# A gated mix of a state-space scan and an FFN on one core: the first x by DMA transposes, B's first slots loaded at once, and another order of the products

## The chip, the core and the metric

The kernel runs on one core of a Trainium2 chip. The time is the device time of one execution in microseconds (us). Before the change, three runs took 143.34, 143.43 and 144.09 us, a median of 143.43 us.

The engines are named as the profile names them: PE is TensorE's matmuls and PEld its weight loads, DVE is VectorE, ACT is ScalarE, POOL is GpSimd and SP is SyncE, which here only issues DMAs. All times in this document are in us unless ns is written.

## The reference

For 2048 tokens `x` of 448 values the kernel computes a gate, a diagonal complex recurrence (S5) over the tokens, an FFN with SiLU, and mixes the two:

```python
g = sigmoid((x * gate_w).sum(-1, keepdims=True))
# a: state-space part
Lam_bar = exp(dt * Lam)                       # 448 complex numbers, dt = exp(log_dt)
B_bar = ((Lam_bar - 1.0) / Lam)[:, None] * B  # 448 x 448 complex
Bu = x @ B_bar.T
h[t] = Lam_bar * h[t - 1] + Bu[t]             # over the 2048 tokens
a = 2.0 * (h @ C.T).real + x * Dskip
# b: FFN, 448 -> 1792 -> 448
b = silu(x @ w1) @ w2
out = g * a + (1 - g) * b                     # bfloat16
```

## The kernel before

**Tiling.** The tokens are cut into four chunks of 512 (`CH`), each of four blocks of 128. The 448 complex states are laid out as seven slots of 128 rows: slots 0 to 2 and half of slot 3 hold the real parts, the other half of slot 3 and slots 4 to 6 the imaginary parts. An eighth slot of `U` and of `Gb` is slot 3 with its halves swapped.

**Per chunk.** Every chunk goes through these stages:

- *Products with 64 rows.* `bu(tc, s)` makes slot s of B times x, `f1(tc, fb)` makes one of 14 blocks of 128 FFN units. Both contract over 448 = 7 x 64 rows, so `step(ta, tb)` runs two of them as a pair, one in each half of PE's rows: eight matmuls of 64 rows and 512 columns that open the pair (`begin`), and six that close it (`end`, issued by `close()` when the next step has begun, or by a call of its own). There are 42 steps. What closes a pair adds the evictions: `U` by ACT or DVE (L631, L633), the FFN's SiLU by ACT into `aT` (L692).
- *Lanes* (`lanes(tc)`, all DVE but for the copies): `U` is turned by the tables `COS` and `SIN` (L652), seven real scans of 512 run over the tokens (L665), their results are copied to `Gb` by ACT (L671) or POOL (L669, the slots in `GP`), and turned back into `H` (L652). The state passed to the next chunk is `gin`, from small POOL and DVE operations.
- *FFN outputs.* `ffn2(tb)` makes one block of 128 tokens from 14 matmuls (L703), and ACT scales it by 1-g into `Tb` (L707).
- *Readouts.* `readout(tb)` multiplies `H` by the converted C, `CP`, with seven matmuls (L731), and DVE adds `tf`, which is x*D*g plus `Tb`, and stores it (L721, L735).
- `gates(tc)` makes g with PE (L774), ACT (L779) and POOL (L780, L781); `skip(tc)` multiplies x by D (L713).

**Before the first product.** x of chunk 0 is loaded as it lies (`xnat`, L356, first on SP), transposed by PE in four groups of four (`x_transposes`, L441) and copied to `xT` by DVE (L447) and ACT (L449). x of the later chunks comes by DMA transposes (`load_xt`, L370), two for a load: columns 0 to 383, and 320 to 447. B is loaded in four pieces into `Bnat` (in `Tb`'s place), transposed by PE (`b_transposes`, L468) and copied to `BT` by DVE (L477) and ACT (L475), for slots 0 and 1, then 4 to 6, then 2 and 3. Four rows of parameters (`prm`, loaded on ACT's queue) are transposed by PE (L487, L489) into `pc`; from it come the phases `ph`, the tables `SIN` and `COS` (DVE, POOL and ACT, L523 to L548), and the small factors: the turn by 512 tokens (`s8`, `c8`, `CC`, `SS`, `SX`) and the factors of C (`sc1`, `sc2`), made by a row of tiny POOL operations (L562 to L589). `idle(n)` runs matmuls on zeros (L425).

**C.** Two DMA transposes bring C into `CT` (L389, also in `Tb`'s place), and `readout_weights(k)` converts it with the small factors: two ACT operations (L757, L759) and two DVE operations (L761, L764) for each of k = 0 to 2, and eight PE transposes, one ACT and one DVE operation for k = 3.

**The order.** The program isn't run in the order of its lines. `Plan` collects every operation with its reads and writes, a cost in us and a priority. `Plan.order()` then places them in time by those costs: each engine takes the operation that can start first, and of equal ones that with the lowest priority number. Only PE keeps the order in which its operations were added; that order is written out by hand at the end of the function (L800 to L868). PSUM's eight banks are given out by the same planner. `Waits` then turns the result into one list for each engine with semaphore waits, and each engine runs its own list strictly in order. A wrong cost therefore changes nothing but the order; an operation placed too early blocks what stands behind it on its engine.

The hand-written order before begins so:

```python
BU(0, (0, 1))
b_transposes(B456, ["Bn3"], 0, False)
b_transposes(B456, ["Bn3"], 1, True)
b_transposes(B23, ["Bn0", "Bn1", "Bn2"], 0, False)
b_transposes(B23, ["Bn0", "Bn1", "Bn2"], 1, True)
gates(0)
BU(0, (4, 5), (6, 2))
step(bu(0, 3), f1(0, 7))
F1(0, (0, 8), (1, 9), (2, 10), (3, 11), (4, 12), (5, 13))
```

After chunk 0 it alternates: the steps of a chunk, its four FFN outputs, with the readouts of the chunk before in between.

Of the kernel before, what the change touches and what calls it, by code (L numbers as in the profile page):

```python
# [17 lines left out]
CH = 512  # L18
# [28 lines left out]
class Plan:  # L47
# [6 lines left out]
    SWITCH = 0.10  # L54

# [46 lines left out]
    def order(self):  # L102
# [28 lines left out]
        while len(done) < len(ops):  # L131
# [20 lines left out]
            if o.sem is not None:  # L152
                free[o.eng] = t + o.cost
                if o.bytes > 4096:
                    pipe = max(pipe, t + 1.5) + o.bytes / 260e3
                    o.end = pipe + 0.4
                else:
                    o.end = t + 3.4
            else:
                extra = 0.0  # L160
                if o.eng == "pe":
                    extra = self.SWITCH if o.rows != rows else 0.0
                    rows = o.rows
                free[o.eng] = o.end = t + o.cost + extra
# [97 lines left out]
def bass_gated_mix__ssm_conv_s5__dense_activation_silu__prompt_kernel(nc, A_x, A_Lambda_re, A_Lambda_im, A_B_re, A_B_im, A_C_re, A_C_im,  # L262
               A_log_dt, A_Dskip, B_x, B_w1, B_w2, gate_w, out):
    with ExitStack() as ctx:
# [90 lines left out]
        def load(q, dst, src, name, nbytes, prio, reads=()):  # L355
            P.add(q, lambda e: e.dma_start(dst, src), list(reads), [name], 0.55 if q == "sp" else 0.3, prio, sem(), nbytes)  # L356
# [9 lines left out]
        def load_xt(tc, n, prio, cost, reads=()):  # L366

            rows = slice(tc * CH, (tc + n) * CH)
            for k, (o, c) in enumerate(((slice(0, 3), slice(0, 384)), (slice(3, 4), slice(320, 448)))):
                P.add("sp", lambda e, o=o, c=c: e.dma_start_transpose(xT[:, o, rows], x2[rows, c]), list(reads),  # L370
                      [f"xT{t}{k}" for t in range(tc, tc + n)], cost[k], prio + k, sem(), n * CH * (1100, 500)[k])

        load_x(0, 0)
        load("sp", Bnat[:, 0:3, :], A_B_re[0:384, :].rearrange("(s p) d -> p s d", p=128), "Bn0", 384 * 896, 1)
        load("sp", Bnat[:, 4:7, :], A_B_im[0:384, :].rearrange("(s p) d -> p s d", p=128), "Bn3", 384 * 896, 2)
        load("sp", Bnat[0:64, 3, :], A_B_re[384:448, :], "Bn1", 64 * 896, 3)
        load("sp", Bnat[64:128, 3, :], A_B_im[384:448, :], "Bn2", 64 * 896, 4)
        for h, (c0, c1) in enumerate(((0, 384), (384, 896))):
            w = w1s[:, :, :].rearrange("p b (q f) -> p b q f", q=2)
            for b in range(3):  # L380
                load("sp", w[:, b, :, c0:c1], B_w1[128 * b:128 * b + 128, :].rearrange("p (q f) -> p q f", q=2)[:, :, c0:c1],
                     f"w1{h}{b}", 128 * 4 * (c1 - c0), 5 + h)
            load("sp", w[64:128, 3, :, c0:c1], B_w1[384:448, :].rearrange("p (q f) -> p q f", q=2)[:, :, c0:c1],
                 f"w1{h}3", 64 * 4 * (c1 - c0), 5 + h)
            load("sp", w1s[0:64, 3, c0:c1], B_w1[320:384, c0:c1], f"w1{h}4", 64 * 2 * (c1 - c0), 5 + h)
        load("sp", w2s[:, :, :], B_w2.rearrange("(fb p) d -> p fb d", p=128), "w2", F_FF * 896, 8)
        load_xt(1, 1, 9, (3.0, 5.0))
        def load_ct(k, dst, src, cost, prio):
            P.add("sp", lambda e: e.dma_start_transpose(dst, src), [], [f"Cn{k}"], cost, prio, sem(), 448 * 800)  # L389


        load_ct(0, CT[:, 0:3, :], A_C_re[:, 0:384], 2.0, 11)
        load_ct(1, CT[:, 3:6, :], A_C_im[:, 0:384], 2.0, 12)
# [3 lines left out]
        def late_loads():  # L397
            load_xt(2, 2, 16, (6.0, 1.4), ["Gb7a", "Gb7b"])
# [3 lines left out]
            for tc in range(1, NCH):  # L402
                load_x(tc, 18 + tc, ["Gb7b"])
# [11 lines left out]
        ACT(lambda e: e.preload_act_table(AF.Exp), [], ["tbl"], 1.3, 4)  # L415


        DVE(lambda e: e.memset(PB[:, 0, :], 0.0), [], ["PB0"], 0.2, 0)  # L418

        def idle(n):  # L420
# [6 lines left out]
            P.add("pe", mm, ["PB0"], [tk], 0.107 * n)  # L427

        idle(15)


        def x_transposes(h, n):

            tk = Ps()

            def mm(pe):
                for q in range(2):
                    for b in range(2):
                        o = (q * 2 + b) * 128
                        c = XCOL[2 * n + q]  # L440
                        r = pe.transpose(bk16(tk)[:, o:o + 128], xnat[:, 2 * h + b, c:c + 128], ident[:, :])  # L441
                return r
            P.add("pe", mm, ["xn0", "ident"], [tk], 0.24)
            dst = xT[:, 2 * n:2 * n + 2, 256 * h:256 * h + 256]
            src = lambda: bk16(tk)[:, 0:512].rearrange("p (q n) -> p q n", q=2)
            if n == 0:
                DVE(lambda e: e.tensor_copy(dst, src()), [tk], [f"xT00{h}"], 0.42, 0)  # L447
            else:
                ACT(lambda e: e.activation(dst, src(), AF.Copy), [tk], [f"xT01{h}"], act_cost(512), 0)  # L449

        for h in range(2):
            for n in range(2):
                x_transposes(h, n)

        def xr(tc):
            return [f"xT{tc}{k}" for k in (range(2) if tc else ("00", "01", "10", "11"))]

        def b_transposes(slots, reads, h, to_act):
# [11 lines left out]
            P.add("pe", mm, reads + ["ident"], [tk], 0.06 * 2 * n)  # L470
# [10 lines left out]

        prmn = [f"prm{k}" for k in range(4)]
# [9 lines left out]
        b_transposes(B01, ["Bn0"], 0, False)  # L492
        b_transposes(B01, ["Bn0"], 1, True)
        idle(2)
# [59 lines left out]
        DVE(lambda e: e.tensor_single_scalar(ph[:, 4:8], ph[:, 0:4], 512.0, ALU.mult), ["ph"], ["ph5"], 0.2, 12)  # L554
        DVE(nearest(phk[:, 4:8], ph[:, 4:8]), ["ph5"], ["phk5"], 0.2, 12)
        DVE(minus(ph[:, 4:8], ph[:, 4:8], phk[:, 4:8]), ["ph5", "phk5"], ["ph5"], 0.2, 12)
        ACT(lambda e: e.activation(s8[:, :], ph[:, :], AF.Sin, scale=TURN), ["ph", "ph5", "tbl"], ["s8"], 0.25, 12)
        ACT(lambda e: e.activation(pha[:, :], ph[:, :], AF.Abs), ["ph", "ph5", "tbl"], ["pha"], 0.25, 12)
        ACT(lambda e: e.activation(c8[:, :], pha[:, :], AF.Sin, bias=hpi[:, :], scale=-TURN), ["pha", "hpi", "tbl"], ["c8"], 0.3, 12)

        def pt(o, a, b, op, r, w):
            POOL(lambda e: e.tensor_tensor(o, a, b, op), r, w, 0.15, 20)  # L562
        nr, ni, m1, m2, inv, a1, a2, a3 = (c[:, :] for c in cw)
        pt(nr, rc[:, :], c8[:, 0:4], ALU.mult, ["rc", "c8"], ["nr"])
        POOL(lambda e: e.tensor_single_scalar(nr, nr, -1.0, ALU.add), ["nr"], ["nr"], 0.15, 20)
# [5 lines left out]
        POOL(lambda e: e.tensor_single_scalar(inv, inv, 2.0, ALU.mult), ["inv"], ["inv"], 0.15, 20)  # L571
# [8 lines left out]
        POOL(lambda e: e.tensor_copy(sc1[:, 0:3], a1[:, 0:3]), ["a1"], ["sc1"], 0.1, 20)  # L580
        pt(sc1[:, 3:4], a1[:, 3:4], sgn[:, :], ALU.mult, ["a1", "sgn", "sc1"], ["sc1"])
        POOL(lambda e: e.tensor_single_scalar(sc1[:, 4:7], a1[:, 0:3], -1.0, ALU.mult), ["a1", "sc1"], ["sc1"], 0.1, 20)
        POOL(lambda e: e.tensor_single_scalar(sc2[:, :], a3, -1.0, ALU.mult), ["a3"], ["sc2"], 0.1, 20)
        POOL(lambda e: e.tensor_copy(CC[:, 0:4], c8[:, 4:8]), ["c8"], ["CC"], 0.1, 14)
        POOL(lambda e: e.tensor_copy(CC[:, 4:7], c8[:, 4:7]), ["c8", "CC"], ["CC"], 0.1, 14)
        POOL(lambda e: e.tensor_copy(SS[:, 0:3], s8[:, 4:7]), ["s8"], ["SS"], 0.1, 14)
        POOL(lambda e: e.tensor_single_scalar(SS[:, 4:7], s8[:, 4:7], -1.0, ALU.mult), ["s8", "SS"], ["SS"], 0.1, 14)
        pt(SS[:, 3:4], s8[:, 7:8], sgn[:, :], ALU.mult, ["s8", "sgn", "SS"], ["SS"])
        POOL(lambda e: e.tensor_single_scalar(SX[:, :], SS[:, 3:4], -1.0, ALU.mult), ["SS"], ["SX"], 0.1, 14)  # L589

        def half_steps(pe, a, b, lo, hi, start):
            for i in range(len(lo)):
                for p0, (w, xc, tk, c0), k in ((0, a, lo[i]), (64, b, hi[i])):
                    r = pe.matmul(bk(tk), w[p0:p0 + 64, k, c0:c0 + 128], xT[p0:p0 + 64, k, xc:xc + CH],  # L599
                                  start=(start and i == 0), stop=(not start and i == 2))  # L600
            return r

        open_pair = []

        def step(ta, tb):

            (wa, xa, ca, ra, ea), (wb, xb, cb, rb, eb) = ta, tb
            a, b = Ps("pair"), Ps("pair")
            begin = lambda pe: half_steps(pe, (wa, xa, a, ca), (wb, xb, b, cb), (0, 1, 2, 3), (0, 1, 2, 3), True)
            end = lambda pe: half_steps(pe, (wb, xb, b, cb), (wa, xa, a, ca), (0, 1, 2), (0, 1, 3), False)  # L610
            reads = ra + rb

            def evict(a, b):
                ea(a)
                eb(b)
            P.add("pe", begin, reads, [a, b], 0.866, rows=64)
            if open_pair:
                close()
            open_pair.append((end, reads, a, b, evict))

        def close():
            end0, reads0, a0, b0, evict0 = open_pair.pop()
            P.add("pe", end0, reads0, [], 0.65, acc=[a0, b0], rows=64)
            evict0(a0, b0)

        GP = ((), (0, 1), (0, 1), ())


        def u_out(s, tk, on_dve=False):
            if on_dve:  # L630
                DVE(lambda e: e.tensor_copy(U[:, s, :], bk(tk)), [tk], [f"U{s}"], dve_cost(512), 2)  # L631
            else:
                ACT(lambda e: e.activation(U[:, s, :], bk(tk), AF.Copy), [tk], [f"U{s}"], act_cost(512), 4)  # L633

        def bu(tc, s):
            def evict(tk):
# [267 lines left out]
```

## Time and profile before

| | |
|---|---|
| median of three runs | 143.43 us (143.34 to 144.09) |
| the profiled execution | 143.92 us |
| its span, from the first instruction to the last | 142.0 us |
| PE busy, share of the span | 97% |
| DVE busy | 89% |
| ACT busy | 56% |
| POOL busy | 24% |
| first product starts | 7.88 us |
| HBM read, written | 6.25 MB, 1.84 MB |

The profile counts time from the first instruction. Its page gives busy times and the costliest groups of instructions; the chain of waits goes back from the last instruction to what released each; a timeline lists instructions of one engine by start and duration, merged where neighbours are alike, with the idle time before them in brackets. Matmuls are pipelined, so their durations overlap: the time that one costs in a row of many is the distance from start to start. For DMAs the profile tells when an engine issued one, how long the issue took and when it landed.

### The profile page before, as it was taken

Reading aid. Unit: us, or ns where it says so; the run is one execution under the profiler, and the core shown is the slowest. Engines: PE = TensorE matmul, PEld = TensorE weight load, DVE = VectorE, ACT = ScalarE, POOL = GpSimd, SP = SyncE. Lnnn points to the kernel's source line nnn. Section 1 sums busy time; section 2 is a strip of 40 time slices with the busy share of each in tenths; the row PEclk is TensorE's granted clock in tenths of the full one; section 3 lists DMA queues with packets and bytes.
Section 4 is the critical chain, followed back from the end, with each engine's and each line's share of the span. In section 5 each row is a group of like instructions: output and inputs, shape, how many; then the busy total and the mean of one; then the engine's idle time right before and its main releaser. Section 6 shows DMA issues by size and latency. Waiting matters only on the chain.

```text
span 142.0 us, 2706 instructions
## 1 busy us (share of the span) xinstructions
PE 137.6 (97%) x1069; PEld 70.6 (50%) x1069; DVE 126.1 (89%) x145; ACT 79.1 (56%) x148; POOL 34.2 (24%) x66
## 2 busy tenths in 40 slices
PE   6989999999999999999999999999999999999993
PEld 4855555544444544444555554444455555555552
DVE  0399999998899299999999999999999999899393
ACT  3386698798965494889811014898721355411100
POOL 7184000089009520443450002542000000000000
PEclk9999999999999999999999999999999999999999
DMA  4989969201947600101000102000001021000113
GB/s 133 331 258 290 314 133 201 33 0 39 239 103 188 229 5 0 37 0 42 2 31 1 41 29 69 18 18 5 0 30 34 0 69 37 31 1 32 32 65 99
DMA packets 21108, 11.44 MB, mean 81 GB/s; under 512 B 11492, under 2 KB 21096, under 8 KB 21096
## 3 DMA queue, kind: packets, MB, share of 16 engines
q1 hardware_dynamic: 21088, 11.27, 30.5%
q8 instruction: 8, 0.13, 0.4%
q14 instruction: 4, 0.03, 0.1%
q10 hardware_dynamic: 8, 0.00, 0.0%
HBM read 6.25 MB, written 1.84 MB: 57 GB/s over the span
## 4 chain that ended last, share of the span: by engine, by line
PE 96%; DVE 1%; ACT 1%; POOL 1%; issue 0%
PE ps L599 45%; PE ps L703 30%; PE ps L731 15%; PE ps L425 2%; PE ps L441 1%; PE ps L774 1%; ACT BT L475 1%; PE ps L468 1%; POOL cw L562 0%; DVE ot L735 0%; PE ps L751 0%; DVE PB L418 0%; POOL gwc L497 0%; DVE pc L495 0%; DVE cw L570 0%
## 5 line engine op out<-in xcount | busy, mean ns | idle before, releaser
L599 PE MATMUL ps<-xT,w1s 64*128 64x512 bf16 x392 | 47.4, 376 | 0.0
L703 PE MATMUL ps<-w2s,aT 128*128 128x448 bf16 x224 | 44.7, 352 | 0.0
L692 ACT ACTIVATE aT<-ps 128x512 bf16<-128x512 f32 x56 | 30.0, 601 | 5.3 <-PE ps L599 5.2
L599 PEld LDWEIGHTS ps<-xT,w1s 64*128 64x128 bf16 x392 | 21.0, 94 | 22.7 <-issue 0.7
L703 PEld LDWEIGHTS ps<-w2s,aT 128*128 128x128 bf16 x224 | 21.7, 98 | 20.3 <-issue 0.4
L665 DVE TENSOR_TENSOR_SCAN Gf<-rc,gin,PA 128x512 f32<-128x512 f32 x21 | 26.8, 1322 | 0.0
L599 PE MATMUL ps<-xT,BT 64*128 64x512 bf16 x196 | 25.9, 376 | 0.7 <-DVE ph L511 0.6
L707 ACT ACTIVATE Tb<-ps,g 128x448 bf16<-128x448 f32 x16 | 10.1, 633 | 28.0 <-PE ps L703 21.4
L731 PE MATMUL ps<-CP,H 128*128 128x448 bf16 (+1 forms) x119 | 23.2, 341 | 0.0
L671 ACT ACTIVATE Gb<-Gf 128x512 bf16<-128x512 f32 x24 | 14.7, 630 | 8.4 <-DVE Gf L665 8.3
L599 PEld LDWEIGHTS ps<-xT,BT 64*128 64x128 bf16 x196 | 10.7, 94 | 12.1 <-DVE phk L508 0.8
L731 PEld LDWEIGHTS ps<-CP,H 128*128 128x128 bf16 x119 | 11.5, 98 | 9.8 <-issue 0.4
L633 ACT ACTIVATE U<-ps 128x512 bf16<-128x512 f32 x24 | 13.3, 592 | 2.2 <-PE ps L599 2.2
L735 DVE SCALAR_TENSOR_TENSOR ot<-ps,g,tf 128x448 bf16<-128x448 f32 (+1 forms) x17 | 11.1, 650 | 3.2 <-issue 2.2
L669 POOL CAST Gb<-Gf 128x512 bf16<-128x512 f32 x4 | 6.1, 1518 | 23.0 <-DVE Gf L665 23.0
L721 DVE SCALAR_TENSOR_TENSOR tf<-xnat,g,Tb 128x448 f32<-128x448 bf16 x16 | 10.6, 674 | 0.1
L652 DVE TENSOR_TENSOR PB<-Gb,SIN 128x1536 bf16<-128x1536 bf16 (+1 forms) x8 | 8.6, 1087 | 1.2 <-ACT Gb L671 1.1
L652 DVE TENSOR_TENSOR PB<-U,SIN 128x2048 bf16<-128x2048 bf16 (+1 forms) x8 | 8.6, 1080 | 0.0
L652 DVE TENSOR_TENSOR PA<-U,COS 128x3584 bf16<-128x3584 bf16 x4 | 8.1, 2020 | 0.2
L652 DVE TENSOR_TENSOR PA<-PA,PB 128x3584 bf16<-128x3584 bf16 x4 | 8.1, 2018 | 0.0
L652 DVE TENSOR_TENSOR H<-PA,PB 128x3584 bf16<-128x3584 bf16 x4 | 8.1, 2014 | 0.0
L652 DVE TENSOR_TENSOR PA<-Gb,COS 128x3584 bf16<-128x3584 bf16 x4 | 8.1, 2014 | 0.0
(97 smaller groups left out, 100.5 us busy)
## 6 DMA issues: line engine op xcount, KB each, us to landing
xnat<-in_A_x_dram SPq DMA_DIRECT2D x4, 448.0 KB, 6.1
out_dram<-ot SPq DMA_DIRECT2D x15, 112.0 KB, 1.7
w2s<-in_B_w_dram SPq DMA_DIRECT2D x1, 1568.0 KB, 9.3
w1s<-in_B_w_dram SPq DMA_DIRECT2D x3, 256.0 KB, 4.6
w1s<-in_B_w_dram SPq DMA_DIRECT2D x3, 192.0 KB, 4.3
Gb<-Gb SPq DMA_DIRECT2D x8, 64.0 KB, 1.9
U<-U SPq DMA_DIRECT2D x6, 64.0 KB, 2.0
Tb<-in_A_B_re_dram SPq DMA_DIRECT2D x1, 336.0 KB, 3.7
```

Of the source, the lines that this page charges most:

```text
L599: r = pe.matmul(bk(tk), w[p0:p0 + 64, k, c0:c0 + 128], xT[p0:p0 + 64, k, xc:xc + CH], start=(start and i == 0), stop=(not start and i == 2))
L633: ACT(lambda e: e.activation(U[:, s, :], bk(tk), AF.Copy), [tk], [f"U{s}"], act_cost(512), 4)
L652: return DVE(lambda e: e.tensor_tensor(o, a, b, op), r, w, dve_cost(n, 2), prio)
L665: DVE(lambda e, s=s, b=b, init=init: e.tensor_tensor_scan(Gf[:, s, :], rc[:, b:b + 1].to_broadcast([128, CH]), PA[:, s, :], init, ALU.mult ...
L669: POOL(lambda e, s=s: e.tensor_copy(Gb[:, s, :], Gf[:, s, :]), [f"Gf{s}"], [f"Gb{s}"], 0.75, 8)
L671: ACT(lambda e, s=s: e.activation(Gb[:, s, :], Gf[:, s, :], AF.Copy), [f"Gf{s}"], [f"Gb{s}"], act_cost(512), 4)
L692: ACT(lambda e: e.activation(aT[tc % 2][:, fb, :], bk(tk), AF.Silu), [tk, "tbl"], [f"aT{tc % 2}_{fb}"], act_cost(512), 3)
L703: r = pe.matmul(bk(tk)[:, 0:D_MOD], aT[tc % 2][:, fb, o:o + 128], w2s[:, fb, :], start=(fb == 0), stop=(fb == NFB - 1))
L707: ACT(lambda e, tk=tk: e.activation(Tb[:, tb, :], bk(tk)[:, 0:D_MOD], AF.Copy, scale=g1[:, tb:tb + 1]), [tk, f"g1_{tc}"], [f"Tb{tb}"] + [f ...
L721: DVE(lambda e: e.scalar_tensor_tensor(tf[tb % 2][:, :], xnat[:, tb, :], g[:, tb:tb + 1], Tb[:, tb, :], ALU.mult, ALU.add), [f"xn{tc}", f" ...
L731: r = pe.matmul(bk(tk)[:, 0:n], Ht[:, s, o:o + 128], CP[:, s, c], start=(s == 0), stop=(s == NSLOT - 1))
L735: DVE(lambda e, tk=tk, c=c, n=n: e.scalar_tensor_tensor(ot[tb % 3][:, c], bk(tk)[:, 0:n], g[:, tb:tb + 1], tf[tb % 2][:, c], ALU.mult, ALU ...
```

## The change

The edits, in the order of the program:

- The planner frees ACT 0.10 and DVE 0.08 before an operation's end, and many costs are set anew (DMA issues, transposes, POOL's small operations). This changes orders, not work.
- x of chunk 0 comes by two DMA transposes, first on SP; the PE transposes of x and their copies are gone. `xnat` of chunk 0 is loaded with the other chunks' in `late_loads`.
- B's slots 0 and 1 are one load, first on ACT's queue ahead of the parameters; slot 2 is a load of its own. Both of their copies to `BT` are DVE's. w1 comes in eight loads instead of ten, in the same two halves.
- The small factors get early priorities; copies of `Gb` move to POOL for chunk 0 (slots 0 and 1) and chunk 3 (slot 0).
- `readout_weights` gets other priorities and stands after the first three FFN outputs.
- The hand-written order of the products is another one from the first step on.

```diff
-        load_x(0, 0)
-        load("sp", Bnat[:, 0:3, :], A_B_re[0:384, :].rearrange("(s p) d -> p s d", p=128), "Bn0", 384 * 896, 1)
+        load("act", Bnat[:, 0:2, :], A_B_re[0:256, :].rearrange("(s p) d -> p s d", p=128), "Bn0", 256 * 896, -1)
+        load_xt(0, 1, 0, (1.45, 0.7))
         load("sp", Bnat[:, 4:7, :], A_B_im[0:384, :].rearrange("(s p) d -> p s d", p=128), "Bn3", 384 * 896, 2)
+        load("sp", Bnat[:, 2, :], A_B_re[256:384, :], "Bn4", 128 * 896, 3)
...
-            for tc in range(1, NCH):
+            for tc in range(NCH):
                 load_x(tc, 18 + tc, ["Gb7b"])
...
-        idle(15)
-        for h in range(2):
-            for n in range(2):
-                x_transposes(h, n)
+        idle(12, 0.213)
...
+        b_transposes(B01, ["Bn0"], 0, False)
+        b_transposes(B01, ["Bn0"], 1, False)
+        idle(4, 0.213)
...
         P.add("pe", prm_t, prmn + ["ident"], [tk], 0.3)
-        b_transposes(B01, ["Bn0"], 0, False)
-        b_transposes(B01, ["Bn0"], 1, True)
-        idle(2)
+        step(bu(0, 0), bu(0, 1))
+        b_transposes(B456, ["Bn3"], 0, False)
+        b_transposes(B456, ["Bn3"], 1, True)
...
-        GP = ((), (0, 1), (0, 1), ())
+        GP = ((0, 1), (0, 1), (0, 1), (0,))
```

The order that follows in the changed kernel (its lines as they stand, some joined):

```python
gates(0)
b_transposes(B23, ["Bn4", "Bn1", "Bn2"], 0, False); close()
b_transposes(B23, ["Bn4", "Bn1", "Bn2"], 1, True)
BU(0, (4, 5), (6, 2)); F1(0, (0, 8)); step(bu(0, 3), f1(0, 7))
F1(0, (5, 13), (4, 12), (3, 11), (2, 10)); lanes(0)
F1(0, (1, 9)); F1(1, (1, 7)); late_loads()
step(f1(0, 6), f1(1, 13)); F1(1, (2, 8)); BU(1, (0, 1), (6, 2), (4, 5)); skip(0)
F2(0, 1, 2); readout_weights(2); close()
F1(1, (4, 10)); readout_weights(0); readout_weights(1)
step(f1(1, 0), bu(1, 3)); close(); F1(1, (5, 11), (3, 9)); lanes(1)
BU(2, (6, 2)); F2(3); gates(3); gates(1); readout_weights(3)
F1(2, (2, 10)); F1(1, (6, 12)); BU(2, (4, 5)); F1(2, (5, 13))
step(bu(2, 3), f1(2, 7)); F1(2, (3, 11), (0, 8))
C(0, 1); F2(6, 5); close()
F1(2, (1, 9)); BU(2, (0, 1)); skip(1); BU(3, (0, 1)); C(2, 3); F2(4); lanes(2)
gates(2); F2(7); F1(3, (5, 11), (2, 8)); step(f1(3, 0), bu(3, 3)); F1(3, (6, 12))
BU(3, (4, 5), (6, 2)); F1(3, (4, 10)); step(f1(2, 6), f1(3, 13))
F1(3, (3, 9)); F1(2, (4, 12)); F1(3, (1, 7)); skip(2); close()
C(4); skip(3); F2(8, 13, 9); C(5); F2(14); C(6, 7, 8); F2(11); C(9); F2(12, 10); C(10)
lanes(3); F2(15); C(11, 12, 13, 14, 15)
```

## The prediction

> **What bounds the kernel now.** First the head of the page: the span and each engine's busy share. Then the chain of waits in order of time, which says where TensorE (PE) ever waited.
>
> ```profile
> span 142.0 us, 2706 instructions
> ...
> PE 137.6 (97%) x1069; PEld 70.6 (50%) x1069; DVE 126.1 (89%) x145; ACT 79.1 (56%) x148; POOL 34.2 (24%) x66
> ```
>
> ```profile
> 7.90 1.02 PE ps L599 x8
> 8.92 0.79 PE ps L468 x12
> 9.71 0.02 issue
> 9.74 0.82 ACT BT L475
> 10.56 0.14 issue
> 10.69 18.95 PE ps L599 x174
> ```
>
> The second fence is the start of the products: the first half step (L599) starts at 7.88, B's transposes (L468) and the gate of chunk 0 follow, PE waits from about 10.4 for ACT's copy of B (L475), and from 10.69 on the chain stays on PE until 139.5, where 2.4 us of eviction and storing end the span. Between 10.69 and 139.54 the pieces are PE's alone. The work there, at the row prices, is 580 half-height matmuls at 0.1089 (18.95/174), 16 FFN outputs at 2.65, 16 readouts at 1.33, three gates and one C transpose: 63.2+42.4+21.2+1.4+0.4 = 128.6 of 128.85 us. So the order of the products holds no idle time to win. All that a change can win lies ahead of 10.69, and it can lose anywhere.
>
> What keeps the first product until 7.88 is seen in the timeline of PE:
>
> ```profile
> 1.18 3.38 PE L425 MATMUL ps<-PB 128*128 128x256 bf16 x15 [1.18 <-DVE PB L418]
> 4.35 1.91 PE L441 MATMUL ps<-ident,xnat 128*128 128x128 bf16 x16
> 6.20 0.23 PE L487 MATMUL ps<-ident,prm 4*128 4x4 bf16 x3
> ...
> 6.49 0.62 PE L468 MATMUL ps<-ident,Tb 128*128 128x128 bf16 x8
> ```
>
> Warm-up matmuls, 16 transposes of x, five of the parameters, eight of B's slots 0 and 1, whose copy on ACT ends at 7.74.
>
> **Step 1, x by DMA.** Removed: 16 PE transposes, two DVE copies (0.42 each), two ACT copies (0.60). Added: two DMA transposes as the first issues on SP. The trace has six such, at other places:
>
> ```profile
> 10.71 7.29 SPq L370 DMA_TRANSPOSE xT<-in_A_x_dram  x1
> ```
>
> ```profile
> 18.05 1.25 SPq L370 DMA_TRANSPOSE xT<-in_A_x_dram  x1
> 19.34 1.33 SPq L389 DMA_TRANSPOSE Tb<-in_A_C_re_dram  x1
> ```
>
> ```profile
> DMA to landing us min/median/max: 3.7/5.5/10.1
> ```
>
> The last line is for xT's four; C's two took 4.4 each. The 10.1 stood behind the 1568 KB of w2, which landed at 19.3; from 17.5 to 19.0 the 16 engines moved only 29 GB/s, so a transpose beside a plain transfer can stall. The nearest rows for an empty queue are C's: 448 rows in 4.4. x has 512 rows and a second, smaller transpose behind it. Issued at 0.73, the first should land at 5.1 and the second (issue at about 2.2, 3.7 as at 18.05) at 5.9. B's first 224 KB go out on ACT's queue at the same time, 0.7 us at the 323 GB/s of the stretch 2 to 6: bounds 5.2 (shared with nothing) to 6.6. The far bound is 0.73+10.1 = 10.8.
>
> **Step 2, B's slots 0 and 1 and the parameters.** B's load landed 3.7 after its issue at 1.25 with x ahead of it; now 0.72 plus at most 3.7, so by 4.4. Eight transposes at the early 0.107 (0.9) and two DVE copies of 0.42 put BT at 5.4 to 5.8. The parameters go out one ACT issue later (0.52); before, they were there by 6.20, so at the latest 6.72, and 0.35 of transposes makes 7.1. The first product therefore starts between 5.3 and 7.1; I take **6.2**, where x decides: -1.68 against 7.88. Behind that new wait on x stand, on PE, B's other transposes and the gate of chunk 0, and behind those ACT's and DVE's copies of B; the parameters' transposes stand ahead of it, so DVE's phases don't wait for x.
>
> The rest of the head costs nothing. Warm-up matmuls are 12 and 4 instead of 15 and 2, ahead of loads that come later. ACT's table load starts 0.52 later, at 2.7, for an Exp at 6.8. x's plain load of chunk 0 (0.47 on SP) moves behind 41 on the same queue; its neighbours there took 5.8 to 7.1, so it lands by 50, and the first readout reads it at about 62.
>
> **Step 3, the head in its new order.** Before, from the first product to 10.69: half step 0.97, 20 transposes 1.13, gate 0.42, wait 0.29, and the close of the pair (0.65) still to come: 3.46. After: 0.97, 12 transposes 0.68, gate 0.42, four transposes 0.23, close 0.65, four transposes 0.23, and three changes between half and full rows at 0.10 (an FFN output after half steps takes 2.75, after readouts 2.65): 3.48. The later order has two more such changes than before: +0.2. ACT's copy of B is again late, since the table load (1.28) and the three small activations (0.7) that now come early stand ahead of it: +0.2, bounds 0 to 0.7.
>
> **Step 4, small factors early, C's conversions later.** This takes away an idle stretch of DVE, not of PE:
>
> ```profile
> DVE CP L761 <- ACT ct L757: 3.1, 1, 3.1
> ```
>
> DVE stands in order, and all of chunk 1 waited behind that CP. The three early operations on DVE cost it 0.45 in the phases. Worth nothing on the path: the last H ends at 130.08 and its first readout starts at 134.2 (132.89 plus one readout), 4.1 us of cover.
>
> ```profile
> 128.07 2.01 DVE L652 TENSOR_TENSOR H<-PA,PB 128x3584 bf16<-128x3584 bf16 x1
> ```
>
> **Step 5, the searched order.** I added up PE's row prices along it. The parts with thin cover, if the first product is at 6.2: w1's first part is read at about 12.1; SP reaches its last issue at about 7.5 (two transposes 2.5, four of B at 0.58, three of w1 at 0.65), and w1's DMAs took 3.5 to 5.0, so 11.0 to 12.5. Its second part is read at 15.1 and lands at 13.8 to 15.1. Chunk 1's xT is read at 22.7; before it landed at 21.78, w2 now goes out some 0.5 later: 22.0 to 22.5. So the head can't gain much more than I take, since xT would be late next. Of the later parts: U's slots 0 and 1 of chunk 2 come at about 76, after two readouts and two FFN outputs; DVE's lanes of chunk 2 began at 75.73 before and needed 54.3 from there to the last H, so 130.3, for a readout at about 132.9. Cover 2.6. Seven copies of Gb on GpSimd at 1.52 instead of four, with more of its small factors done before, lie beside scans of 1.2 each. I price these at 0.
>
> **Sum.** -1.68 +0.02 +0.2 +0.2 = -1.26. The profiled execution took 143.92 (span 142.0 and 1.92 around it), so 142.7 by it; the median of the three runs is 143.43, so **142.2**. About 0.5% (0.7 us) is what a measurement of this kernel can tell from no change.
>
> **Rivals.**
> *Forecast*, first product at 5.7 to 6.7, no later wait over 0.3: 141.7 to 142.7. Chance 0.52.
> *Better*, x at 5.3 and xT of chunk 1 by 21.8: -0.9 more, 141.3. For it: C's transposes landed in 4.4 with others around them. Against: B's load beside it. 0.08.
> *Half rate.* Up to 5.95 PE started a 128-column transpose each 0.106 (L441: (1.91-0.31)/15), from 6.49 each 0.057 (L468), although the page's clock digits show 9 throughout. PE had then run without rest since 1.18. The new head has two rests, before B's landing (3.7 to 4.4) and before x. If PE counts anew from 4.3, the full rate comes 5.1 later, at 9.4, and the 3.2 us of products before it cost 1.6 more: 143.8; half of that is 143.0, which I take. 0.10.
> The Trainium skill (TensorE: Matmul & The Clock Gate, What's actually happening) says that the rate doubles after one whole busy window of about 3.4 us, and that the windows run freely, not from the kernel's start. By that the full rate comes between 4.6 and 8.0 here, the trace's 6.0 to 6.5 agrees, and at worst the estimate is 0.9 more than the forecast, 143.1; before, everything ahead of 7.88 hid it.
> *Thin cover*, w1 or xT of chunk 1 later by 1.0 than I read, because plain transfers behind a transpose start slowly (U's 64 KB took 3.6 at 37.5 behind one, 1.9 alone): PE waits as much, 143.2. 0.15.
> *Slower: x's transpose stalls* on an engine that still has B's packets, as xT did on w2's. Place: the first wait of PE. From a first product at 7.4 on the gain is gone; halfway between C's 4.4 and xT's 10.1, it lands at 8.0 and with the second transpose's 0.6 PE starts at 8.6: 142.2+2.4 = 144.6. 0.09.
> *Slower: DVE late.* If U's slots of chunk 2 come over 2.6 us later than 76, or DVE idles as much, each further us is one of PE's; 4.5 us would give 144.1. 0.06.
>
> **Numbers.** Faster by over 0.5%: 0.60 (forecast and better). Within: 0.25 (half rate, thin cover). Slower: 0.15. The range reaches from 141.1 to 144.1 and leaves out the far end of the stalled x.
>
> **What would show it.** The first L599 start (7.88 now) near 6.2 and ended by xT's DMA; no wait of PE over 0.3 between 10 and 137; the last PE piece ending near 138.3; the 3.1 us row of CP gone with no change of the end; H's last end at least 1 us before its readout. Wrong would be a first product after 7.4, or a new PE wait on w1, xT, U or H of over a microsecond.

## The result, and the profile after

| | before | after |
|---|---|---|
| median, same chip, 22 runs each | 143.72 us (143.04 to 144.42) | 143.09 us (142.68 to 144.04) |
| ratio after to before, of the means, with its 95% interval | | 0.9962 [0.9944, 0.9979] |
| profiled execution, its span | 143.92, 142.0 | 143.37, 141.3 |
| first product starts | 7.88 | 6.06 |
| last piece of PE ends | 139.54 | 138.89 |

The changed kernel is 0.38% faster, not the 0.86% that was forecast (142.2 against 143.43). One of the 22 runs before took 208.08, far outside the others, and is in neither the range nor the ratio.

The head of the page after:

```profile
span 141.3 us, 2663 instructions
...
PE 136.3 (96%) x1052; PEld 67.3 (48%) x1052; DVE 126.7 (90%) x144; ACT 77.0 (54%) x142; POOL 37.5 (27%) x69
```

PE is busy 1.3 us less, but the span is only 0.7 shorter: PE waits more than before. The timeline of PE in the new head (start, duration, engine and line; idle before in brackets) shows where. L476 is now the half step, L456 B's transposes, L767 the gate, L535 and L537 the transposes of the parameters:

```profile
5.80 0.21 PE L535 MATMUL ps<-ident,prm 4*128 4x4 bf16 x3 [0.86 <-DMA prm<-in_gate_w_dram]
5.93 0.19 PE L537 MATMUL ps<-ident,prm 4*64 4x4 bf16 x2
6.06 1.04 PE L476 MATMUL ps<-xT,BT 64*128 64x512 bf16 x8
7.37 0.84 PE L456 MATMUL ps<-ident,Tb 128*128 128x128 bf16 x12 [0.27 <-DMA Tb<-in_A_B_im_dram]
8.05 0.54 PE L767 MATMUL ps<-gwc,xT 128*128 128x1 bf16 x16
8.89 0.38 PE L456 MATMUL ps<-ident,Tb 128*128 128x128 bf16 x4 [0.30 <-DMA Tb<-in_A_B_im_dram]
9.21 0.82 PE L476 MATMUL ps<-xT,BT 64*128 64x512 bf16 x6
9.96 0.40 PE L456 MATMUL ps<-ident,Tb 128*128 128x128 bf16 x4
10.29 1.04 PE L476 MATMUL ps<-xT,BT 64*128 64x512 bf16 x8
```

The first product is where the forecast had it (6.2), and x's two transposes landed where it had them (5.18 and 5.84, for 5.1 and 5.9). But x did not decide the start: PE's last wait before it is for the parameters, and the product follows their transposes at once, 0.2 after x was there. From there to the second step (10.29) the head takes 4.23 instead of the forecast's 3.48 (3.68 with its 0.2 for ACT's copy of B): PE waits twice for pieces of B, which land at 7.32 and 8.76. Before, all of B had landed by 6.86. The chain of waits runs through SP's issues to that last piece:

```profile
0.73 1.40 SPq L374
...
2.17 1.29 SPq L374
...
3.52 0.61 SPq L358
...
5.30 3.45 DMA Tb<-in_A_B_im_dram
```

The two transposes hold SP until 3.46, so B's later pieces go out at 3.52 to 5.30 (before: 1.80 to 2.93). From issue to landing they take 3.2 to 3.8, and took 3.9 to 4.7 before, so what has grown is the time until the issue. In the stretch 4 to 6, though, the DMA engines also move less. Before and after (busy time of five engines, PE's clock, the DMA engines' busy share, GB/s):

```profile
4.00:6.00 2.00, 2.00 (x19) 1.88 (x17) 0.55 (x2) 0.55 (x1) 0.00 (x0) 1.00 1.06 344
```

```profile
4.00:6.00 2.00, 1.14 (x15) 0.85 (x13) 0.75 (x2) 0.32 (x1) 0.00 (x0) 1.00 1.02 211
```

The engines are as busy (1.02 against 1.06) and move 39% less. The Trainium skill (DMA: Bandwidth & Descriptors, Latency and other measured facts) gives a DMA transpose with a non-contiguous middle dimension 261 GB/s, some 30% below a contiguous one. This stretch mixes transposes with plain loads, and no run here shows the rate of the transposes alone, so whether the loss is of that kind stays open.

DVE's 3.1 us stall before a conversion of C is gone, and the end did not notice it, as forecast: the last H is done at 125.66 and is first read at about 133.6.

```profile
123.63 2.03 DVE L645 TENSOR_TENSOR H<-PA,PB 128x3584 bf16<-128x3584 bf16 x1
```

But the conversion of C's last part (L754) is now in PE's way: it frees a PSUM bank late, and between the two PE pieces there are 0.25 more than a step needs (0.46 from start to start, less 0.21). The chain of waits leads from this conversion back over DVE's work, some of ACT's between, to B's landing at 8.76.

```profile
54.70 0.67 DVE L754 SCALAR_TENSOR_TENSOR CP<-ps,sc,ct 128x448 bf16<-128x448 bf16 x1
```

```profile
53.67 1.68 PE L476 MATMUL ps<-xT,w1s 64*128 64x512 bf16 x14
55.43 0.82 PE L476 MATMUL ps<-xT,BT 64*128 64x512 bf16 x6
```

The changed kernel was run twice more, with other kernels beside it.

> The changed kernel itself once more, beside the three others on one chip. Its profile showed PE's matmuls at full rate from 4.25 on (every 0.107 us a half-height matmul), so its head was the good case. If the clock's windows of 3.4 us run freely, other executions are at half rate up to 7.6 or, where PE rested too long in a window, up to 11: times in two groups, some 0.7 to 1.2 apart, ratio to the kernel before 0.994 to 0.999. If the clock has no part in it: one group within 0.4, ratio 0.995 to 0.997.

> The changed kernel again, beside the following three on one chip. Both theories: ratio 0.995 to 0.998, and a wait on w1's second half in the profiled execution wherever its last piece lands after 15.1 us.

Measured: 143.06 (142.46 to 144.37), ratio 0.9968 [0.9939, 0.9998], and 143.39 (142.85 to 144.43), ratio 0.9988 [0.996, 1.0016]. The first 12 times spread over 1.9 with no gap above 0.4, so they are neither the two groups nor the one narrow group that the first expectation named; the second ratio lies just above its range, with the wait on w1 that it named. In both profiled executions the head was shorter (3.85), and PE waited at 15 to 16.5 instead. The timeline of PE in the third:

```profile
14.78 0.38 PE L476 MATMUL ps<-xT,BT 64*128 64x512 bf16 x1
14.78 1.02 PE L476 MATMUL ps<-xT,w1s 64*128 64x512 bf16 x7
16.47 1.24 PE L476 MATMUL ps<-xT,w1s 64*128 64x512 bf16 x9 [0.67 <-ACT aT L685]
```

and its rows of DMA issues (KB, median us to landing) for the last two pieces of w1's second half:

```profile
w1s<-in_B_w_dram SPq DMA_DIRECT2D x1, 128.0 KB, 5.6
...
w1s<-in_B_w_dram SPq DMA_DIRECT2D x1, 64.0 KB, 5.8
```

The view names ACT, but the instruction waits for several semaphores, w1's among them. The 64 KB were issued at 10.30 and landed at 16.12; PE starts 0.35 later. Six executions (here and below) have this wait, and in each PE starts 0.35 or 0.36 after that landing: 15.96 and 16.31, 16.12 and 16.47, 16.05 and 16.40, 15.29 and 15.64, 15.78 and 16.14, 15.73 and 16.08. ACT's end does not fit all of them: in the execution with 15.29 and 15.64 ACT had ended its last operation at 14.68.

### The profile page after: what moved, and what is told of

It is laid out like the page before. It is cut to its first block, busy times and chain, and to the rows that moved or that the text cites. A ratio compares the mean times of both kernels' runs of the same rounds, so it can differ in the third digit from the quotient of the medians.

```text
span 141.3 us, 2663 instructions
## 1 busy us (share of the span) xinstructions
PE 136.3 (96%) x1052; PEld 67.3 (48%) x1052; DVE 126.7 (90%) x144; ACT 77.0 (54%) x142; POOL 37.5 (27%) x69
## 3 DMA queue, kind: packets, MB, share of 16 engines
HBM read 6.25 MB, written 1.84 MB: 57 GB/s over the span
## 4 chain that ended last, share of the span: by engine, by line
PE 59%; DVE 25%; issue 6%; SPq 3%; DMA 2%; ACT 2%; ACTq 0%
PE ps L696 23%; PE ps L476 21%; PE ps L724 15%; DVE PA L645 6%; DVE Gf L658 4%; DVE PB L645 4%; DMA Tb<-in_A_B_im_dram 2%; SPq L374 2%; DVE U L505 2%; DVE CP L754 2%; DVE Gf L593 1%; SPq L358 1%; DVE xnat L706 1%; DVE Gf L575 1%; DVE CP L757 1%
## 5 line engine op out<-in xcount | busy, mean ns | idle before, releaser
L476 PE MATMUL ps<-xT,w1s 64*128 64x512 bf16 x392 | 48.0, 376 | 0.0
L696 PE MATMUL ps<-w2s,aT 128*128 128x448 bf16 x224 | 44.0, 353 | 0.0
L476 PEld LDWEIGHTS ps<-xT,w1s 64*128 64x128 bf16 x392 | 20.0, 94 | 23.5 <-issue 0.7
L476 PE MATMUL ps<-xT,BT 64*128 64x512 bf16 x196 | 27.8, 377 | 0.1
L724 PE MATMUL ps<-CP,H 128*128 128x448 bf16 (+1 forms) x119 | 22.5, 342 | 0.0
L662 POOL CAST Gb<-Gf 128x512 bf16<-128x512 f32 x7 | 10.0, 1432 | 31.7 <-DVE Gf L658 31.7
L664 ACT ACTIVATE Gb<-Gf 128x512 bf16<-128x512 f32 x21 | 13.3, 632 | 8.6 <-DVE Gf L658 8.5
L476 PEld LDWEIGHTS ps<-xT,BT 64*128 64x128 bf16 x196 | 10.4, 94 | 11.6 <-DVE CP L754 0.6
L773 POOL TENSOR_SCALAR g<-th 128x4 f32<-128x4 f32 x4 | 5.0, 1241 | 28.5 <-ACT th L772 28.5
L645 DVE TENSOR_TENSOR PB<-U,SIN 128x1536 bf16<-128x1536 bf16 (+1 forms) x8 | 8.5, 1085 | 0.2
L658 DVE TENSOR_TENSOR_SCAN Gf<-rc,PA 128x512 f32<-128x512 f32 x7 | 8.6, 1265 | 0.0
```

Of the source, the lines that this page charges most:

```text
L645: return DVE(lambda e: e.tensor_tensor(o, a, b, op), r, w, dve_cost(n, 2), prio)
L658: DVE(lambda e, s=s, b=b, init=init: e.tensor_tensor_scan(Gf[:, s, :], rc[:, b:b + 1].to_broadcast([128, CH]), PA[:, s, :], init, ALU.mult ...
L662: POOL(lambda e, s=s: e.tensor_copy(Gb[:, s, :], Gf[:, s, :]), [f"Gf{s}"], [f"Gb{s}"], 1.5, 8)
L664: ACT(lambda e, s=s: e.activation(Gb[:, s, :], Gf[:, s, :], AF.Copy), [f"Gf{s}"], [f"Gb{s}"], act_cost(512), 4)
L696: r = pe.matmul(bk(tk)[:, 0:D_MOD], aT[tc % 2][:, fb, o:o + 128], w2s[:, fb, :], start=(fb == 0), stop=(fb == NFB - 1))
L724: r = pe.matmul(bk(tk)[:, 0:n], Ht[:, s, o:o + 128], CP[:, s, c], start=(s == 0), stop=(s == NSLOT - 1))
```

## The experiments

**Half of the change alone.** Theory on record: the head carries the gain, and the searched order by itself costs 0.2 to 0.4. The first kernel has the new head and, from `BU(0, (4, 5))` on, the old order; the second has the old head (x loaded and transposed by PE, the old loads of B) and the new order.

```diff
-BU(0, (4, 5), (6, 2)); F1(0, (0, 8)); step(bu(0, 3), f1(0, 7)) ...   # after
+BU(0, (4, 5), (6, 2)); step(bu(0, 3), f1(0, 7)); F1(0, (0, 8), (1, 9), ...   # before
```

```diff
-load_xt(0, 1, 0, (1.45, 0.7))
+load_x(0, 0)
+x_transposes(h, n)
```

> The changed kernel's head up to the transposes of slots 2 and 3, then the product order of the kernel before. Main theory: the searched order gains nothing by itself and costs about 0.35 (one wait of 0.25 for a bank that DVE's conversion of C frees, two changes of rows): this one ends 0.2 to 0.4 before the changed kernel, ratio 0.993 to 0.995. Rival (the searched order is needed to keep PE busy behind an earlier head): new waits of 0.3 or more between 11 and 60, ratio 0.997 to 1.000.

> The head of the kernel before (x by PE transposes, four loads of B on SP), then the searched product order and everything else of the changed kernel. Main theory: no gain from the order, 0.2 to 0.4 us lost: ratio to the kernel before 1.001 to 1.003. Rival (the order and the early small factors carry the gain): 0.996 to 0.998, as the whole change.

Measured: 144.62, ratio 1.0082 [1.0047, 1.0117], and 145.2 (6 runs), ratio 1.0103 [1.007, 1.0136]. Each half alone is slower than before, by more than either theory or rival allowed: neither half carries the gain, and together they win. With the old order the longest waits of PE are these (total, times, longest); the second stands at 92:

```profile
PE ps L456 <- DMA Tb<-in_A_B_im_dram: 0.6, 2, 0.4
PE ps L476 <- ACT U L507: 0.6, 1, 0.6
```

With the old head and the new order:

```profile
PE ps L499 <- DVE BT L488: 0.8, 1, 0.8
PE ps L499 <- ACT rc L578: 0.6, 1, 0.6
```

The second of these is no loss against before: it stands ahead of the first product at 7.90, and the kernel before waits 0.56 at the same place.

**B's issues.** Is it SP's queue that makes B late, or the DMA engines?

```diff
-load("sp", Bnat[:, 2, :], ...); load("sp", Bnat[0:64, 3, :], ...); load("sp", Bnat[64:128, 3, :], ...)
+load("act", Bnat[:, 2, :], ...); load("act", Bnat[0:64, 3, :], ...); load("act", Bnat[64:128, 3, :], ...)
```

> B's last three pieces are issued on ACT's queue right behind the parameters, at about 3.0 to 4.2 instead of 4.17 to 5.89 on SP's. If the late landing comes from SP's queue (two transposes of 1.3 to 1.4 us of issue stand ahead), the last piece lands near 7.8 instead of 8.76 and the second wait (0.43) goes: ratio to the kernel before 0.992 to 0.994. Rival (the engines are the limit: they moved 211 GB/s in the two microseconds in which the transposes end, 344 before): it lands between 8.4 and 8.8 all the same, B's piece for slots 4 to 6 lands later than 7.32, ratio 0.995 to 0.998.

Measured: 145.77 (6 runs), ratio 1.0132 [1.009, 1.0174], outside both ranges. The three pieces went out 1.1 to 1.3 us earlier and landed 0.4 to 1.0 earlier, the last of them at 8.40 (8.76); the piece for slots 4 to 6, still on SP, landed at 8.60 (7.32). Its chain:

```profile
3.72 4.88 DMA Tb<-in_A_B_im_dram
8.60 0.05 issue
8.65 1.30 PE ps L456 x12
```

So PE waits for B about as long (0.54, in the changed kernel 0.27 and 0.30): what some pieces gain another loses, as the rival (the DMA engines limit) had it. It is not shown, though, that the engines are the cause: the edit also let w1's loads out 1.6 earlier (from 4.36 on, not 5.93), beside B's, and x's second transpose landed 1.1 later (6.97). Besides, PE fell to half its rate from 8.9 to 12.3 here.

**The close of the first pair, and PE's rate.** The close needs no more of B, so it can fill the first wait; `idle` can fill the rests.

```diff
         step(bu(0, 0), bu(0, 1))
+        close()
         b_transposes(B456, ["Bn3"], 0, False)
...
-        close()
```

```diff
-        idle(4, 0.213)
+        idle(8, 0.213)
```

> Main theory (the head waits for B's later pieces: 0.34 us before the transposes of slots 4 to 6, 0.43 before those of slots 2 and 3, and 0.2 goes into two more changes between half and full rows): with the first pair closed at once, its six matmuls run while B lands and the row changes go. The matmuls of the second step start near 9.4 instead of 10.29, PE ends 0.7 to 0.9 earlier, the ratio to the kernel before is 0.990 to 0.992. Rival 1 (ACT's copy of B holds the second step, not the loads): it starts at 9.9 to 10.3 as now, ratio 0.994 to 0.997. Rival 2 (what the head gains is taken back by later waits of the product order): the second step starts near 9.4, but the end moves by less than 0.3, ratio 0.994 to 0.997.

> The first pair closed at once, as in the earlier run, and 8 matmuls on zeros instead of 4 behind B's first transposes. In the profile of the earlier run PE was at half rate until 10.31, which hid what the edit does. Theory: at full rate the second step starts near 9.5 instead of 10.3, and PE ends 0.7 earlier: ratio to the kernel before 0.987 to 0.992. Rival (the close is no use because ACT's and DVE's copies of B come at the same time as before): second step at 10.0 or later even at full rate, ratio 0.994 or more.

> Adds matmuls on zeros where PE rests in the new head: 8 instead of 4 behind B's first transposes, 3 behind the first half step, 3 behind the gate of chunk 0; nothing else is changed. Clock theory (rests in the head keep PE at half rate, or bring it back there, in part of the executions): the slow group goes, median 0.3 to 0.8 below the changed kernel's on the same chip, ratio to the kernel before 0.990 to 0.995. Rival (PE waits for loads alone, the clock is full in any case): the same as the changed kernel, or 0.1 to 0.3 slower, since the fillers end after the loads have landed.

> Takes the 4 matmuls on zeros behind B's first transposes away, so that PE rests from about 4.4 until the parameters have landed at 5.7. Nothing that the products need is changed. Clock theory: more executions reach the first products at half rate and stay there until about 10: ratio to the kernel before 1.000 to 1.010. Rival (loads alone): no change against the changed kernel, ratio 0.995 to 0.997.

`close_first` is the first edit, `close_first_fill` both; `fill` has the second and two `idle(3)` in the head, `rest` has no second `idle` at all. Measured: `close_first` 144.25, ratio 1.0016 [0.9985, 1.0048]; `close_first_fill` 143.39, 0.997 [0.9951, 0.999]; `fill` 143.34, 0.9985 [0.9964, 1.0006]; `rest` 143.65, 0.9987 [0.9965, 1.0008]. None beat the change. In the profiled executions of `close_first` and `rest`, PE ran at half rate until 10.3, so `close_first` says nothing of the close; in those of `fill` and `close_first_fill` it had the full rate before the first product (6.21 and 6.58). In `close_first_fill` the second step came at 10.28, not at the theory's 9.5: the fillers had put the first product at 6.58, and the rival (10.0 or later) holds. The ranges (the changed kernel's was 1.9 us on that chip, those of the two with fillers 1.1 and 0.9) suggest that fillers keep PE from the half rate; with one profiled execution each that is not shown. Their medians are 0.3 above the change's there, as the rival of `fill` said.

**w1's second half read later, and B's late pieces taken away.** Theory: PE waits first for B's late pieces, then for w1's.

```diff
-F1(0, (5, 13), (4, 12), (3, 11), (2, 10)); lanes(0); F1(0, (1, 9))
+F1(0, (2, 10), (1, 9), (5, 13), (4, 12)); lanes(0); F1(0, (3, 11))
```

```diff
-load("sp", Bnat[:, 4:7, :], ...)   # and slots 2, 3
+load("sp", Bx[:, 2:5, :], ...)
+DVE(lambda e: e.memset(Bnat[:, 2:7, :], 0.0), ...)
```

> The FFN outputs that read w1's second half stand about 3 us later in the order (read at about 18 us instead of 15.1); nothing else differs. Theory (w1's second half lands at 13.7 to 16.0 and holds PE in a part of the executions): no wait of PE on w1, the times' top is lower, the median 0.2 to 0.4 us below the changed kernel's, ratio to the kernel before 0.993 to 0.996. Rival (that wait was of one execution and does not weigh in the median): ratio 0.996 to 0.998, as the changed kernel has it.

> B's slots 2 to 6 are loaded by the same four transfers into a spare tile, and the slots themselves are zeroed early by DVE: the DMA traffic and PE's work stay, PE's wait on the late pieces of B goes. It leaves out these slots of B, so the products are those of a B with zeros there. Theory (the head lost its 0.4 to 0.8 us to B's late landings): the second half step (the close) starts near 9.5 instead of 10.0 to 10.3, ratio to the kernel before 0.990 to 0.993. Rival (the copies of B on ACT and DVE, as the prediction had it, are late next): the second half step not before 9.9, ratio 0.994 or more.

> Both edits: B's slots 2 to 6 to a spare tile (they are left out of the products, zeros in their place) and the outputs on w1's second half 3 us later. Theory (late B and late w1 are what the forecast missed): ratio 0.988 to 0.991, the forecast's size. Rival (the missing half microsecond lies elsewhere: PE's rate, or the waits behind DVE's copies): ratio 0.993 or more.

> The outputs on w1's second half later, and the close of the first pair ahead of gate 0, so that B's last two pieces are needed 0.6 to 1.0 us later and PE has work in the place of its second wait. Nothing is left out. Theory: the second half step starts at about 9.0, the transposes of B's last pieces follow it without a wait, ratio 0.991 to 0.994. Rival (B's order is not what counts, or the earlier close waits for something else): ratio as that of the kernel with the w1 edit alone, 0.994 to 0.997.

Measured: `w1_later` 143.68, ratio 1.0003 [0.9975, 1.0031]; `b_elsewhere` 143.3, 0.9988 [0.9953, 1.0024]; `b_elsewhere_w1` 143.51, 0.9987 [0.9958, 1.0017]; `w1_later_close` 143.33, 0.9981 [0.9951, 1.0011]. All four theories missed their ratios, for two reasons. The first edit did not do what it says: output 10 reads the second half too (column 384 of its part), so the read stayed at its place, and all four have the wait at 15 to 16.4. And `b_elsewhere` showed what the wait on B was worth: the second step came 3.45 after the first product, the forecast's 3.48, and PE then lost 0.41 of it to w1.

**The same, done truly.** The pair (1, 9) reads w1's first half only. `xt_before_w2` was to move chunk 1's two transposes ahead of w2's load.

```diff
-F1(0, (5, 13), (4, 12), (3, 11), (2, 10)); lanes(0); F1(0, (1, 9))
+F1(0, (1, 9), (5, 13), (4, 12), (3, 11)); lanes(0); F1(0, (2, 10))
```

```diff
-load_xt(1, 1, 9, (7.7, 1.3))
+load_xt(1, 1, 7.4, (3.0, 1.3))
```

> The pair (1, 9), which reads w1's first half alone, goes ahead of (5, 13), and (2, 10) takes its old place: w1's second half is read 1.5 us later, at about 16.6 instead of 15.1. Theory (w1's second half and then chunk 1's xT bound the head): no wait at 15 to 17, but up to 0.6 us of it comes back at 21 to 23 as a wait on xT of chunk 1, whose landing doesn't move (22.0 to 22.8); 0.1 to 0.5 us below the changed kernel, ratio to the kernel before 0.992 to 0.996. Rival (the loss is PE's rate in the head): as the changed kernel.

> The two transposes of chunk 1's x are issued ahead of w2's load instead of behind it; the order on PE is the changed kernel's. Theory: xT of chunk 1 lands by 18 instead of 22.4, w2 by 23, which is read at 32; the wait at 15 stays, so ratio 0.995 to 0.998, or worse if the transposes delay w1's second half, whose last piece then lands after 16. Rival (xT's late landing is what the change lost): ratio 0.991 to 0.994.

> Both edits: w1's second half read 1.5 us later and chunk 1's xT ahead of w2. Theory (two transfers in a row bound the head, w1's second half and xT): no wait of PE over 0.3 us between 11 and 50 and 0.4 to 0.8 us below the changed kernel on the same chip, ratio to the kernel before 0.989 to 0.993, near the forecast's 0.991. Rival (neither is what the change lost): ratio 0.995 or more.

Measured, beside the third run of the change (0.9988): `w1_one_later` 143.04 (142.69 to 143.96), ratio 0.9966 [0.9941, 0.9991]; `xt_before_w2` 143.38, 0.9983 [0.9958, 1.0008]; `w1_and_xt` 143.2, 0.9979 [0.9951, 1.0007]. With (1, 9) first the wait at 15 is gone, and PE's last piece starts 0.73 earlier than the change's in the profiled pair; the medians differ by 0.35, within the intervals. The ratio of `w1_one_later` lies just above its theory's range, that of `w1_and_xt` misses 0.989 to 0.993. But the xT edit did only half of what it says: the first transpose went out ahead of w2 (10.81, w2 at 13.04), the second behind it, and landed at 22.52, in `w1_and_xt` at 21.48 (the changed kernel: 21.96 to 22.96). What an early xT is worth was thus not tested. The profiled execution of `xt_before_w2`, whose head is the change's, ran at half rate until about 10:

```profile
6.24 1.89 PE L476 MATMUL ps<-xT,BT 64*128 64x512 bf16 x8
8.06 1.46 PE L456 MATMUL ps<-ident,Tb 128*128 128x128 bf16 x12
```

Eight half matmuls take 1.89 instead of 1.04. That head took 5.08, and as PE was late there was no wait on w1.

**Both waits away, and the nearest that keeps the work.** The first kernel is `b_elsewhere` with the last order; the second is that order with the close ahead of gate 0, and leaves nothing out.

```diff
+close()
 gates(0)
 b_transposes(B23, ["Bn4", "Bn1", "Bn2"], 0, False)
-close()
```

> B's slots 2 to 6 go to a spare tile and are zeros in the products (left out), and w1's second half is read truly one pair later. Theory (the two landings make up what the forecast missed): second half step near 9.5, no wait at 15 to 17, ratio to the kernel before 0.989 to 0.993, the forecast's 0.991. Rival (taking away the one wait uncovers the next, ACT's or DVE's copies or xT of chunk 1, and PE's rate in part of the executions): ratio 0.994 or more, with the wait in its new place.

> The whole computation; w1's second half read one pair later, and the close of the first pair ahead of gate 0, so that B's last pieces are needed later. Theory: B's waits shrink by 0.2 to 0.4 and no wait at 15 to 17: ratio 0.992 to 0.996, at or below that of the w1 edit alone (0.9966). Rival (the next wait takes it): 0.996 or more.

Measured: `b_w1_one_later` 142.79 (142.41 to 142.99, 8 runs), ratio 0.9936 [0.991, 0.9963]; `w1_one_later_close` 143.0 (142.53 to 143.3, 12 runs), ratio 0.9944 [0.9921, 0.9967]. The first, PE's timeline:

```profile
6.04 1.04 PE L478 MATMUL ps<-xT,BT 64*128 64x512 bf16 x8
7.01 0.84 PE L458 MATMUL ps<-ident,Tb 128*128 128x128 bf16 x12
...
9.50 1.69 PE L478 MATMUL ps<-xT,BT 64*128 64x512 bf16 x14
```

The second step stands at 9.50, as the theory said. The ratio is just above its 0.989 to 0.993, and the interval reaches down to the forecast's 0.991. In the second kernel, whose ratio is as its theory said, the head takes 3.55, near the forecast's 3.48 with all of B in it, and the next thin cover shows at once, chunk 1's xT:

```profile
21.98 0.31 PEld L476 LDWEIGHTS ps<-xT,w1s 64*128 64x128 bf16 x4
23.25 0.79 PEld L476 LDWEIGHTS ps<-xT,w1s 64*128 64x128 bf16 x10 [0.95 <-DMA xT<-in_A_x_dram]
```

It landed at 23.19 and cost 0.65. This kernel has the lowest median of those that keep the whole computation, and is the best version found; its interval overlaps the change's.

## Why the prediction was wrong

The shift of PE's last piece against before, in the profiled executions, adds up from the places where PE lost time (us; the head's loss is its length less 3.46, a later wait is start to start less the usual 0.22; the rest is what remains to the measured sum):

| kernel | first product | head | w1 | later waits | rest | sum |
|---|---|---|---|---|---|---|
| forecast | -1.68 | +0.22 | 0 | 0 | +0.2 | -1.26 |
| changed | -1.82 | +0.77 | 0 | +0.31 | +0.09 | -0.65 |
| changed, again | -1.75 | +0.39 | +0.92 | 0 | +0.08 | -0.36 |
| changed, third | -1.49 | +0.39 | +0.83 | 0 | +0.06 | -0.21 |
| `w1_one_later` | -1.64 | +0.30 | 0 | +0.32 | +0.08 | -0.94 |
| `b_w1_one_later` | -1.84 | -0.01 | 0 | +0.43 | +0.08 | -1.34 |

- **Steps 1 and 2, right in time, not in what decides.** The first product came at 6.06, 6.13 and 6.39 for 6.2. The step said that x decides and that xT's DMA ends the wait; in all three PE waited last for the parameters (0.86, 0.45 and 0.64), and the product followed their transposes, about 0.2 after xT's last landing (5.84, 5.92 and 6.18). The difference is small: in `b_on_act`, where PE did wait for x, the product came 0.10 after the landing (6.97 and 7.07), so x alone would have given about 5.9 in the first (an estimate). The step had bounded the parameters at 7.1 and not put them beside x.
- **Step 3, the step that failed first.** Its +0.02 is right for PE's work alone: without the wait on B the head takes 3.45. Its +0.2 for ACT's late copy of B was the wrong thing: no wait on ACT's copy showed. What is late are B's slots 2 to 6, which stand behind two transposes on SP: +0.39 to +0.77 in the changed kernel, and -0.01 where the products don't wait for them (`b_w1_one_later`). The step priced B's first load and never asked when the others land. How much of the lateness is SP's queue, and how much the DMA engines that move 211 GB/s instead of 344, stays open.
- **The row changes fit.** +0.2 less the 0.12 of one wait before that is gone (at 63) makes +0.08; the rest column has +0.06 to +0.09.
- **Step 4, right** on the stall; it didn't see that L754 would hold a bank at 55 (0.25), which shows only where PE is early.
- **Step 5, the other failure.** It named w1's second part as thin (read at 15.1, landing 13.8 to 15.1) and priced it at 0. Over the changed kernel's three profiled executions it landed at 14.60, 15.96 and 16.12, and PE came to it at 15.70, 15.40 and 15.65: 0, 0.92 and 0.83 of waiting. The rival *Thin cover*, at 0.15, is what happened in two of three.
- **The rivals.** *Better*, *x's transpose stalls* and *DVE late* did not come. *Half rate* did in one of the eleven profiled executions that have the change's fillers and its order up to gate 0, and in `close_first`, which is the same up to the first half step; its share of the other runs is open. *Thin cover* and *Half rate* did not add: the late PE of `xt_before_w2` found w1 landed.
- **The base.** The three runs shown had a median of 143.43, the 22 beside the change 143.72. Of the 0.9 between 142.2 and 143.09, 0.3 is this; the other 0.6 is what the waits of the table come to in the first profiled execution (-0.65 for -1.26).

Left open: why single runs of both kernels spread over 1.4 us or more on one chip, why neither half of the change wins by itself, and whether w2's load, issued 0.6 after w1's last piece, makes that piece late; with a transpose in between (`xt_before_w2`) it landed at 15.14.

## What to carry to other kernels

When a load is moved ahead, list every later load on the same queue and engines with its new landing time and the time at which it is read; the gain at the front is paid back at the first of them whose cover is thinner than the gain, and then at the next. A series of covers thinner than the gain (here B, w1, xT) is a forecast of its own and not a zero with a note. And an experiment that moves a read later has to be checked against what each moved product reads.

## What the runs showed of the hardware

- In the stretch 4 to 6, DMA engines at about the same busy share (1.02 and 1.06) moved 211 GB/s with two DMA transposes in front and 344 without; in the 17 other executions with the new head it was 208 to 242, in the one with the old head 334.
- In `b_on_act` PE's rate fell to half at 8.9 and rose again at 12.3 (128-column transposes start 0.056, then 0.107, then 0.056 apart), about 3.4 later; the mean granted clock of that run is given as 0.988. The Trainium skill (TensorE: Matmul & The Clock Gate, What's actually happening) has free-running windows of 3413 ns; the trace agrees on the step. In the 3.4 ahead of the fall PE had waited 0.79, 0.33 and 0.54, so rests of 1.7 in all stood ahead of it in this one execution.
- The first matmul that reads w1's last piece, where it waited for it, started 0.35 after the landing, in six executions to within 0.01. It is not a general figure: behind B's pieces PE started 0.05 and 0.13 after (7.32 and 7.37, 8.76 and 8.89).
